# Attention, then a two-layer MLP with split f16 products: the first batch's attention in groups of two units, w_out's bit conversion ahead of the token norms, w_out's scale later, some blocks one step later

## The chip, the cores and the metric

The kernel runs on one core of a Trainium2 chip. A core has a matrix engine (TensorE, "PE" in the profile, with "PEld" for its weight loads), a vector engine (VectorE, "DVE"), a scalar engine (ScalarE, "ACT"), GpSimd ("POOL") and SyncE ("SP", here used to issue DMAs). Each engine works off its own instructions in order; they wait for each other through semaphores. Matmul results go to PSUM, of which this program names the slots "sc" (two of two banks), "mm" (two), "av" and "tr" (one each).

The metric is device time of one execution in microseconds, the median of several runs. Lower is better.

## The reference

```python
scores = scale * np.matmul(q, k.transpose(0, 1, 3, 2)) - np.log(S)
attn = 1.0 / (1.0 + np.exp(-scores))            # a sigmoid, no softmax
attn_out = np.matmul(attn, v)
x = attn_out.transpose(0, 2, 1, 3).reshape(B * S, H * D)
h = x @ w_in
g = h - np.tanh(h)
out = g @ w_out
```

Batch 8, 12 heads, 448 tokens of 64 dimensions each; so x is 3584 x 768, w_in 768 x 2048, w_out 2048 x 768. The weights come as float64 and are converted on the chip.

## The kernel before, in words

**Stages.** Batches are worked one after the other. Batch 0 is special: its attention (`attention32`) and its first MLP product (`moe1_32`) use f32 operands while the weights are still being loaded and converted. Later batches use pairs of f16 (a high and a low half, three products each) in `moe1` and `moe2`. While one batch's second product (`moe2`) runs, the next batch's attention is fed in between as "blocks" of a generator (`stream`).

**Units.** Heads are treated in six pairs j. A unit (j, c) is one slice of 128 key tokens (c = 0, 1, 2) of a pair; c = QT = 3 is the rest of 64 tokens for two pairs at once, so even pairs have four units and odd ones three, 21 in all. A unit is `scores` (PE, into a slot "sc"), `weigh` (sigmoid on ACT, a 128 x 896 tile) and `av` (PE, times v, into an accumulator). When a pair is done `evac_x` copies the accumulator (ACT for even pairs, DVE for odd ones), ACT squares it, POOL adds the squares.

**attention32 before (L625 to L645).** A loop over the 21 units: scores, weigh, then the av of the unit two before, then one step of `weights` (two after a rest unit).

**weights and rest.** Both are generators made by `convert` (L178). A piece of a weight matrix passes through load (SP's DMA), sign (ACT, `conv_sign`), bits (three DVE operations, `conv_bits`, L151 to L155) and end (one PE matmul, `conv_end`, L168 or L172). Each `next` runs one step: every stage for another piece, from the last stage to the first. `weights` is w_in in 24 pieces of 512 KB (five buffers "raw"; the end of a piece comes one step after its bits). The first `rest` is half of w_out in 16 pieces of 384 KB (the end comes two steps after the bits); a second `rest` with the other half runs in batch 0's `moe2`.

**moe1_32 (L741 to L783).** For k = 0 to 7 and e = 0, 1: twelve f32 matmul instructions into "ph" (slot "sc"), then the small things of that step: at (0, 0) the last of `weights`, the token norms (`token_norms`: two matmuls "nm", a DVE reduction); at (0, 1), (1, 0), (1, 1) the sums that give w_in's scale (`w_in_scales`); one `next(self.blocks)` at e = 0 (INIT); then steps of `rest`. After e = 1 comes `mix`: u and th on ACT, then five DVE operations with ACT's squares between (L791 to L809). The last k's mix is left to `first`, which runs it in steps (`tail`) between the first five blocks of batch 1's attention. `w_out_scale(0)` (eight DVE operations, L248 to L255) is issued at the end of moe1_32, ahead of that last mix.

**Blocks.** For two pairs (g, g + 1) there are five blocks: units 0 and 1 of g; units 2 and 3 of g and the norms (ACT squares "sqn") of pair g + 3's q and k; the sums of those norms on PE ("pbn", L297) with the scales and the next K; units 0 and 1 of g + 1; unit 2 of g + 1. BLOCKS0 and BLOCKS1 say after which step of `moe2` a block is issued, for the passes of batch 0 and of batch 1. A step is six matmuls "po" of 384 columns. BLOCKS is the same list for later batches.

**What sets the order.** PE, ACT, DVE and POOL are in a manual schedule: they execute in program order. SP is in it from batch 1 on; in all of batch 0 the framework orders SP's DMA issues by itself. `manual_schedule` leaves the choice of slots and the waits to the framework.

Of the kernel before, what the change touches and what calls it, by code (L numbers as in the profile page):

```python
# [20 lines left out]
D = 64  # L21
QT = 3
# [11 lines left out]
class Builder:  # L34
# [7 lines left out]
    BLOCKS = (8, 11, 16, 19, 20, 24, 27, 32, 35, 36, 40, 43, 48, 51, 52)  # L42
    TAIL = (1, 2, 3, 4, 5)
    ALONE = 11
    BLOCKS0 = (2, 5, 7, 8, 12, 16, 20, 22, 24, 31, 38)
    BLOCKS1 = (4, 6, 7, 10, 13, 16, 19, 20, 24, 27, 32, 35, 36, 40, 43, 48, 51, 52)

    TP = 8
    SHIFT = 4
# [534 lines left out]
    def attention32(self, b, weights, rest):  # L584

        nc = self.nc
        S = self.S
        NP = self.NP
        xs = []
        tags = (("kn", "qn"), ("K", "Q"))  # L590
        self.row = []
        loaded = {}

        def load(j):
            loaded[j] = self.load_qk(b, j, tags[j % 2])
            if j < 2:
                next(weights)
            loaded[j].append(self.load_v(b, j, self.att, "vhl", 3))

        load(0)  # L600
        one = self.sm.tile([P, 1], F32, name="one", tag="m")
        nc.scalar.activation(one, self.nls, AF.Sigmoid)
        next(weights)
        load(1)
        next(weights)
        todo = []
        accs = {}

        def open_acc(j):
            accs[j] = self.ps.tile([P, 512], F32, name="acc", tag="mm", bufs=2)  # L610

        def av():
            j, c, a = todo.pop(0)
            v = loaded[j][2][:, None]
            if c == QT:
                open_acc(j + 1)
                self.av([accs[j], accs[j + 1]], v, a, c, 0)
            else:
                if c == 0 and j % 2 == 0:
                    open_acc(j)  # L620
                self.av([accs[j]], v, a, c, j % 2)
            if c == (QT, QT - 1)[j % 2]:
                xs.append(self.evac_x(j, accs.pop(j), None))

        self.warm(12)  # L625
        order = [(j, c) for j in range(NP) for c in (range(QT) if j % 2 else range(QT + 1))]
        for n, (j, c) in enumerate(order):
            both = (j, j + 1) if c == QT else (j,)
            ps = self.scores([loaded[i][0][:, None] for i in both], [loaded[i][1][:, None] for i in both], c)
            todo.append((j, c, self.weigh(ps, 1.0 / math.sqrt(D))))  # L630
            if n < 2:
                self.warm(4)
            if len(todo) > 2:
                av()
            if c == 1 and j + 2 < NP:
                load(j + 2)
            next(weights)
            if c == QT:
                next(weights)
            if n == len(order) - 1:  # L640
                next(rest)
        while todo:
            av()
            next(weights, None)
            next(rest)  # L645
        self.xs = xs

    def token_norms(self, nm):
# [92 lines left out]
    def moe1_32(self, xs, weights, rest):  # L741


        nc = self.nc
        S = self.S
        self.gs = []
        self.late = []
        for k in range(self.NF // 2):
            ph = self.ps.tile([P, 2, 512], F32, name="ph", tag="sc", bufs=2)
            for e in range(2):  # L750
                f = 2 * k + e
                for c in range(self.NC):
                    nc.tensor.matmul(  # L753
                        ph[:, e, :S],
                        self.where("in", c)[:, f * P : (f + 1) * P],
                        xs[c],
                        start=(c == 0),
                        stop=(c == self.NC - 1),
                    )
                if k == 0 and e == 0:  # L760
                    for _ in weights:
                        pass
                    w = self.w_in_scales()
                    m = self.token_norms(self.ps.tile([P, 512], F32, name="nm0", tag="mm", bufs=2))
                elif k < 2:
                    next(w, None)
                if (k, e) == (1, 1):
                    self.Sg, self.iSg = self.g_scales(m)
                if e == 0 and k in self.INIT:
                    next(self.blocks)  # L770
                for _ in range(3 if k == 0 else 1):
                    next(rest, None)
                if (k, e) == (self.NF // 2 - 1, 1):
                    for _ in rest:
                        pass
                    self.w_out_scale(0)
            g = self.gp.tile([P, 2, 2, S], F16, name="g", tag="g")
            self.gs.append(g)
            self.tail = self.mix(ph[:, :, :S], g, self.ih0, self.ihk0)
            if k == self.NF // 2 - 1:  # L780
                return
            for _ in self.tail:
                pass  # L783
# [140 lines left out]
    def first(self, rest):  # L924

        n = 5
        next(self.tail)
        ahead = [self.split_w_out(0)]
        for k in range(n - 1):
            if k == 2:  # L930
                next(self.blocks)
            next(self.blocks)
            for _ in range(2):
                next(self.tail, None)
            if k == 1:
                next(ahead[0])
            if k == 2:
                self.finish_g()
                next(ahead[0])
        next(ahead[0])  # L940
        next(rest)
        next(ahead[0])
        next(rest)
        assert n + len(self.BLOCKS0) + len(self.BLOCKS1) == 5 * self.NP + len(self.BLOCKS) - self.ALONE
        split = self.split_w_in()
        at, each = self.SPLIT
        events = [(at + k * each, lambda: next(split, None)) for k in range(self.NC * self.NB + 1)]
        events += [(k + 0.5, lambda: next(ahead[0], None)) for k in range(self.NF // 2 - 3)]
        steps = self.NF + 4
        events += [(k * self.CONV, lambda: next(rest, None)) for k in range(1, steps + 1)]  # L950
        at = math.ceil(steps * self.CONV)

        def scale():
            self.w_out_scale(1)
            ahead[0] = self.split_w_out(1)

        events += [(at, scale)] + [(at + 0.5 * k, lambda: next(ahead[0], None)) for k in range(1, self.NF // 2 + 1)]
        self.second(0, self.BLOCKS0, len(self.BLOCKS0) - 1, events)

    def batch(self, b):  # L960
# [15 lines left out]
        if b == 1:  # L976
            alone += len(self.BLOCKS1) - len(self.BLOCKS)
            blocks = self.BLOCKS1
        self.second(b, blocks, alone, events)
# [56 lines left out]
```

## Time and profile before

| | us |
|---|---|
| median of 3 runs | 1209.24 (1207.33 to 1209.73) |
| the profiled execution | 1209.36 |
| its span, first to last instruction | 1207.6 |
| batch 0's attention, first scores to first ph | 6.42 to 58.98 |
| moe1_32, first ph to the first scores of batch 1 | 58.98 to 139.77 |
| busy in the span: PE, DVE, ACT | 1171.3, 917.9, 872.5 |
| mean granted TensorE clock | 0.991 |

A row of the timeline has the start, the duration, engine, line of the program, operation, output tile <- input tiles, shape and count; behind it in brackets, how long the engine was idle before and what it was waiting for. Consecutive equal instructions are merged into a row, so a row's duration is that of its whole run, and matmuls overlap: the pace of PE is read from start to start.

### The profile page before, as it was taken

How to read it: one execution, taken by the hardware profiler on the slowest of the kernel's cores; microseconds unless marked ns; L12 is line 12 of the kernel's file. 1: busy time of each engine (PE TensorE's matmuls, PEld its weight loads, DVE VectorE, ACT ScalarE, POOL GpSimd, SP SyncE). 2: the span in 40 equal slices, each digit the busy share in tenths (PEclk: the TensorE clock that was granted, in tenths of full speed). 3: DMA queues.
4: the chain of work that ended last, by engine and by line, in shares of the span. 5: the costliest groups of instructions: out<-in, count | busy, mean ns of one | idle time of the engine just before them, and what ended most of it. 6: DMA issues, size and time to landing. Idle time of an engine off the chain costs nothing.

```text
span 1207.6 us, 19052 instructions
## 1 busy us (share of the span) xinstructions
PE 1171.3 (97%) x7581; PEld 602.4 (50%) x7581; DVE 917.9 (76%) x1362; ACT 872.5 (72%) x1219; POOL 81.6 (7%) x62
## 2 busy tenths in 40 slices
PE   9899869899999999999999999999999999999998
PEld 2244324455445555555555555555555555555555
DVE  6879888779876798678976798668977789646930
ACT  6757787958888588867878688886887688844820
POOL 0100000000011000110011000210003000210000
PEclk9999899999999999999999999999999999999999
DMA  9832145100022100211012100221002100000000
GB/s 337 303 102 77 46 148 157 59 21 1 18 82 66 51 1 16 73 60 38 1 53 75 57 2 16 66 67 37 1 29 84 60 14 1 29 19 15 1 14 33
DMA packets 34057, 70.43 MB, mean 58 GB/s; under 512 B 3888, under 2 KB 21040, under 8 KB 33968
## 3 DMA queue, kind: packets, MB, share of 16 engines
q1 hardware_dynamic: 33824, 68.99, 17.9%
q8 instruction: 59, 0.97, 0.3%
q14 instruction: 30, 0.25, 0.1%
q10 hardware_dynamic: 144, 0.23, 0.1%
HBM read 58.20 MB, written 11.01 MB: 57 GB/s over the span
## 4 chain that ended last, share of the span: by engine, by line
PE 85%; DVE 7%; ACT 4%; issue 3%; DMA 1%; DVEq 0%; ACTq 0%; SPq 0%
PE ph L723 31%; PE po L836 29%; PE sc L347 8%; PE acc L378 7%; PE por L874 5%; PE ph L753 3%; DMA raw<-moe_w_in 1%; ACT a L358 1%; DVE stb L152 1%; DVE m L795 1%; PE warm L91 1%; DVE g L708 1%; DVE m L806 1%; DVE stb L151 1%; DVE wo L203 1%
## 5 line engine op out<-in xcount | busy, mean ns | idle before, releaser
L836 PE MATMUL po<-wo,g 128*128 128x384 f16 x2304 | 396.4, 327 | 3.2 <-DVE wo L203 1.2
L723 PE MATMUL ph<-xhl,wi 128*128 128x448 f16 x2016 | 382.6, 352 | 0.0
L836 PEld LDWEIGHTS <-g 128*128 128x128 f16 x2304 | 220.2, 99 | 174.1 <-issue 35.9
L723 PEld LDWEIGHTS <-wi 128*128 128x128 f16 x2016 | 196.7, 98 | 185.0 <-issue 1.8
L365 DVE SCALAR_TENSOR_TENSOR ahl<-a,ahl 128x896 f16<-128x896 f32 x126 | 160.6, 1309 | 135.2 <-ACT ahl L364 135.1
L358 ACT ACTIVATE a<-sc,nls,rn 128x896 f32<-128x896 f32 x147 | 156.3, 1091 | 51.3 <-PE sc L347 47.7
L791 ACT ACTIVATE u<-ph,ih 128x896 f32<-128x896 f32 x64 | 64.4, 1006 | 83.3 <-PE ph L723 79.1
L364 ACT ACTIVATE ahl<-a 128x896 f16<-128x896 f32 x126 | 113.1, 940 | 0.6
L347 PE MATMUL sc<-Q,K 64*128 64x448 f16 x1008 | 104.2, 362 | 4.6 <-DVE th L796 2.3
L795 DVE SCALAR_TENSOR_TENSOR m<-ph,ihk,u 128x896 f32<-128x896 f32 x64 | 73.4, 1147 | 29.2 <-ACT th L793 28.8
L707 ACT ACTIVATE g<-m,Sg 128x896 f16<-128x896 f32 x64 | 66.6, 1041 | 36.1 <-DVE m L809 29.1
L809 DVE COPY_PREDICATED m<-u,th 128x896 f32<-128x896 uint32 x64 | 77.1, 1205 | 6.6
L378 PE MATMUL acc<-ahl,vhl 128*64 128x448 f16 (+1 forms) x864 | 81.3, 358 | 0.0
L708 DVE SCALAR_TENSOR_TENSOR g<-m,Sg,g 128x896 f16<-128x896 f32 x64 | 73.3, 1145 | 8.5 <-ACT g L707 8.5
L406 POOL TENSOR_TENSOR x<-x 128x448 f32<-128x448 f32 x24 | 26.4, 1100 | 769.4 <-ACT x L394 769.4
L806 DVE SCALAR_TENSOR_TENSOR m<-q,m 128x896 f32<-128x896 f32 x64 | 69.9, 1093 | 10.8 <-ACT q L805 3.8
L753 PE MATMUL ph<-x,wi 128*128 128x448 f32 x192 | 74.8, 539 | 0.0
L796 DVE SCALAR_TENSOR_TENSOR th<-ph,ih,th 128x896 f32<-128x896 f32 x64 | 73.2, 1143 | 0.0
L808 ACT ACTIVATE u<-u,b 128x896 f32<-128x896 f32 x64 | 66.7, 1043 | 7.3 <-DVE m L795 5.3
L802 DVE SCALAR_TENSOR_TENSOR m<-q,m 128x896 f32<-128x896 f32 x64 | 69.5, 1085 | 0.0
L347 PEld LDWEIGHTS <-K 64*128 64x128 f16 x1008 | 36.4, 98 | 65.0 <-issue 40.4
L874 PE MATMUL por<-wo,g 128*64 128x384 f16 x768 | 65.8, 327 | 1.1 <-ACT o L865 1.1
(127 smaller groups left out, 1154.0 us busy)
## 6 DMA issues: line engine op xcount, KB each, us to landing
raw<-moe_w_in SPq DMA_DIRECT2D x24, 512.0 KB, 6.1
rawo<-moe_w_out SPq DMA_DIRECT2D x32, 384.0 KB, 3.8
knn<-k SPq DMA_DIRECT2D x45, 224.0 KB, 2.5
qnn<-q SPq DMA_DIRECT2D x44, 224.0 KB, 2.6
out<-o SPq DMA_DIRECT2D x21, 384.0 KB, 2.3
vn<-v SPq DMA_DIRECT2D x24, 256.0 KB, 2.9
vn<-v SPq DMA_DIRECT2D x24, 192.0 KB, 2.4
out<-orem SPq DMA_DIRECT2D x16, 96.0 KB, 2.2
```

Of the source, the lines that this page charges most:

```text
L347: self.nc.tensor.matmul(ps[i * m : (i + 1) * m, h, : self.S], K[i][r, w, c * P : c * P + m], Q[i][r, x, :], start=(n == 0), stop=(n == len ...
L358: self.nc.scalar.activation(a[:, 0], ps[:, :, : self.S], AF.Sigmoid, bias=self.nls, scale=scale)
L364: nc.scalar.activation(A[:, 0], a[:, 0], AF.Copy, scale=A_SCALE)
L365: nc.vector.scalar_tensor_tensor(A[:, 1], a[:, 0], A_SCALE, A[:, 0], op0=ALU.mult, op1=ALU.subtract)
L378: self.nc.tensor.matmul(acc[i][h * D : (h + 1) * D, : self.S], v[k, w, 2 * QT + h if half else h * QT + c], A[k, x, h], start=(n == 0 and ...
L708: nc.vector.scalar_tensor_tensor(g[:, 1], m, Sg, g[:, 0], op0=ALU.mult, op1=ALU.subtract)
L723: nc.tensor.matmul(ph[:, e, :S], self.wi[:, c * self.NB + k, part, e * P : (e + 1) * P], xhl[c][:, x, :], start=(i == 0), stop=(i == 3 * s ...
L753: nc.tensor.matmul(ph[:, e, :S], self.where("in", c)[:, f * P : (f + 1) * P], xs[c], start=(c == 0), stop=(c == self.NC - 1),)
L795: V.scalar_tensor_tensor(m, ps, ihk, u, op0=ALU.mult, op1=ALU.mult)
L806: V.scalar_tensor_tensor(m, q2, C2, m, op0=ALU.add, op1=ALU.mult)
L836: nc.tensor.matmul(po[i][:, :H], gs[f // 2][:, x, f % 2, tk * P : (tk + 1) * P], self.wo[:, i * self.NF + f, w], start=(f == 0 and n == 0) ...
L874: nc.tensor.matmul(po[e * D : (e + 1) * D, :H], gs[f // 2][:, x, f % 2, nm:S], self.wo[:, e * self.NF + f, w], start=(f == 0 and n == 0), ...
```

## The change

attention32 takes two units at a time: both scores, both weighs, then all av that were ready before this group (two, none in the first group), then the steps of `weights` of both units. The last group has one unit. After the loop comes one step of `rest`, the last av, and two steps of `rest`, so three as before; the 29th step of `weights` (the end of piece 23) is no longer made here but with "the last of `weights`" in moe1_32.

In moe1_32 the steps of `rest` come directly behind the ph matmuls, ahead of the last of `weights`, the token norms, w_in's sums and the block; and there are two per half at k = 0 instead of three. `w_out_scale(0)` moves behind the first step of the last mix.

In BLOCKS0 the steps 7, 8 and 22 become 8, 9 and 23; in BLOCKS1 6, 7 and 10 become 7, 8 and 11.

```diff
-    BLOCKS0 = (2, 5, 7, 8, 12, 16, 20, 22, 24, 31, 38)
-    BLOCKS1 = (4, 6, 7, 10, 13, 16, 19, 20, 24, 27, 32, 35, 36, 40, 43, 48, 51, 52)
+    BLOCKS0 = (2, 5, 8, 9, 12, 16, 20, 23, 24, 31, 38)
+    BLOCKS1 = (4, 7, 8, 11, 13, 16, 19, 20, 24, 27, 32, 35, 36, 40, 43, 48, 51, 52)
...
-        for n, (j, c) in enumerate(order):
-            both = (j, j + 1) if c == QT else (j,)
-            ps = self.scores([loaded[i][0][:, None] for i in both], [loaded[i][1][:, None] for i in both], c)
-            todo.append((j, c, self.weigh(ps, 1.0 / math.sqrt(D))))
-            if n < 2:
+        for n in range(0, len(order), 2):
+            group = order[n : n + 2]
+            pss = []
+            for j, c in group:
+                both = (j, j + 1) if c == QT else (j,)
+                K, Q = ([loaded[i][x][:, None] for i in both] for x in range(2))
+                pss.append(self.scores(K, Q, c))
+            ready = len(todo)
+            todo += [(j, c, self.weigh(ps, 1.0 / math.sqrt(D))) for (j, c), ps in zip(group, pss)]
+            if n < 4:
                 self.warm(4)
-            if len(todo) > 2:
+            for _ in range(ready):
                 av()
-            if c == 1 and j + 2 < NP:
-                load(j + 2)
-            next(weights)
-            if c == QT:
+            for j, c in group:
+                if c == 1 and j + 2 < NP:
+                    load(j + 2)
                 next(weights)
-            if n == len(order) - 1:
-                next(rest)
+                if c == QT:
+                    next(weights)
+        next(rest)
         while todo:
             av()
-            next(weights, None)
             next(rest)
+        next(rest)
...
                         stop=(c == self.NC - 1),
                     )
+                for _ in range(2 if k == 0 else 1):
+                    next(rest, None)
                 if k == 0 and e == 0:
                     for _ in weights:
                         pass
...
                 if e == 0 and k in self.INIT:
                     next(self.blocks)
-                for _ in range(3 if k == 0 else 1):
-                    next(rest, None)
                 if (k, e) == (self.NF // 2 - 1, 1):
                     for _ in rest:
                         pass
-                    self.w_out_scale(0)
...
         next(self.tail)
+        self.w_out_scale(0)
         ahead = [self.split_w_out(0)]
```

## The prediction

> **What bounds the kernel now.** I read the page's first line and its slices, then a table of windows, then the waits of PE, then the order of time at the places that those name.
>
> ```profile
> span 1207.6 us, 19052 instructions
> ```
>
> ```profile
> 15.37:32.56 17.19, 15.72 (x74) 4.17 (x73) 15.16 (x26) 13.35 (x20) 1.37 (x1) 1.00 0.98 352
> 32.56:49.74 17.18, 15.71 (x74) 4.17 (x73) 15.93 (x26) 14.67 (x21) 2.61 (x2) 1.00 0.91 331
> 59.00:139.77 80.77, 77.33 (x223) 38.35 (x221) 71.26 (x114) 52.98 (x75) 0.00 (x0) 1.00 0.30 85
> 500.00:600.00 100.00, 100.00 (x691) 52.70 (x686) 79.92 (x113) 76.26 (x100) 5.98 (x4) 1.00 0.12 36
> ```
>
> Columns of a window: width, then busy time of PE, PEld, DVE, ACT, POOL, the granted clock, DMA share, GB/s. From about 225 us on PE has no gap worth the name (100.00 of 100), so whatever is won or lost earlier arrives at the end one for one. All that the change touches lies before 330 us. There PE is nearly full too, but so is DVE: in batch 0's attention (two periods of seven units, 17.19 and 17.18 us) DVE is idle only 2.03 and 1.25 us.
>
> ```profile
> PE pbn L297 <- ACT sqn L289: 8.2, 3, 3.8
> PE wl L168 <- DVE stb L152: 8.1, 9, 1.4
> PE cs L172 <- DVE sta L152: 3.3, 3, 1.4
> PE sc L347 <- DVE th L796: 2.3, 1, 2.3
> ```
>
> Total, number of times, longest. These four are what the edits can reach: 21.9 us at most, and 8.2 of it is the sums of norms (pbn) standing in PE's queue before ACT has the squares.
>
> **The change part by part.** First the groups of two in attention32.
>
> ```profile
> 39.12 1.02 PE L347 MATMUL sc<-qnn,knn 64*128 64x448 f32 x4
> 40.08 0.97 PE L378 MATMUL acc<-a,vn 128*64 128x448 f32 x4
> 40.98 0.40 PE L172 MATMUL cs<-sta,identb 128*128 128x512 bf16 x1
> 41.31 1.02 PE L347 MATMUL sc<-qnn,knn 64*128 64x448 f32 x4
> ...
> 80.68 4.67 PE L753 MATMUL ph<-x,wi 128*128 128x448 f32 x12
> 85.19 0.33 PE L168 MATMUL wl<-stb,onesb 128*128 128x384 bf16 x1
> ```
>
> Start to start, scores take 0.96, attention times v 0.90 and cs 0.33: 2.19 us per unit. Twelve f32 matmuls in a row take 4.51, or 0.376 each; four that run two by two would need 0.75. So a change of kind costs up to 0.21 after scores and 0.15 after av, and pairing removes one of each per group: 0.36, in ten groups 3.6 us of PE time. The rows before show no pair of f32 units, so 0 to 3.6 are the bounds of what PE can save. The Trainium skill (TensorEngine Tiling (Array Packing), Key Properties) says that changing the tiling mode drains the TensorE, which names the same gap; by it the sum would be rival 1.
>
> I take it that PE does not collect this, because DVE sets the pace:
>
> ```profile
> 17.39 0.66 ACT L146 ACTIVATE sta<-raw 128x512 f32<-128x512 f32 x1 [1.77 <-DMA raw<-moe_w_in]
> 20.30 0.54 ACT L392 ACTIVATE x<-acc 128x448 f32<-128x448 f32 x1
> 20.88 0.58 ACT L404 ACTIVATE x<-x 128x448 f32<-128x448 f32 x1
> ...
> 18.08 0.43 DVE L151 TENSOR_SCALAR sta<-sta 128x512 uint32<-128x512 uint32 x1 [0.56 <-ACT sta L146]
> 22.52 0.43 DVE L151 TENSOR_SCALAR sta<-sta 128x512 uint32<-128x512 uint32 x1 [0.77 <-ACT sta L146]
> 31.04 0.42 DVE L151 TENSOR_SCALAR sta<-sta 128x512 uint32<-128x512 uint32 x1
> 32.83 0.42 DVE L151 TENSOR_SCALAR sta<-sta 128x512 uint32<-128x512 uint32 x1
> 53.59 0.42 DVE L151 TENSOR_SCALAR sta<-sta 128x512 uint32<-128x512 uint32 x1
> ...
> 58.98 4.78 PE L753 MATMUL ph<-x,wi 128*128 128x448 f32 x12
> ```
>
> One piece of w_in costs DVE 1.79 us (31.04 to 32.83), and PE's cs for a piece needs its bits. Up to piece 5 (18.08) the arrival of the raw weights decides (1.77 us wait at 17.39), with groups or without. From there to piece 22 (53.59) DVE takes 35.5 us, of which I put 1.5 down as idle, between the 0.77 of the row at 22.52 and the 3.3 of the two windows together. In groups, the sign of a piece stands on ACT behind two weighs (0.9 each) and, where an accumulator ends, behind its copy and square (20.30, 20.88: 1.05 together). Walked group by group with a group's PE time of 3.9 us (sc 1.70, av 1.65, cs 0.57), DVE finds nothing to do for 1.6 us at piece 6 (sign ends 17.95 + 2 x 0.9 + 1.05 + 0.65 = 21.5, DVE free at 19.9), 0.65 at the first copy, 0.8 and 0.3 in the middle and 1.3 at piece 22: 4.65 instead of 1.5. Piece 22 then starts at 53.6 + 3.1 = 56.7; its second operation ends 1.15 later, cs and the last av (0.33 + 0.96) end at 59.1. Against 58.98 that is **0**; the last cs, now behind the next stage's first half, no longer makes PE wait here. Bounds: -4.1 us (PE's 3.6 and the 0.5 of the last wait) and +3.
>
> Second, w_out's bits and the small sums in moe1_32. T is the start of the first ph, 58.98.
>
> ```profile
> 64.17 0.62 DVE L652 TENSOR_REDUCE m<-nm 128x1 f32<-128x448 f32 x1 [4.45 <-PE nm L650]
> 72.55 0.35 DVE L151 TENSOR_SCALAR stb<-stb 128x384 uint32<-128x384 uint32 x1
> 74.01 1.15 DVE L795 SCALAR_TENSOR_TENSOR m<-ph,ihk,u 128x896 f32<-128x896 f32 x1
> ...
> 142.10 0.54 DVE L248 TENSOR_REDUCE mo<-wl 128x1 f32<-128x384 f32 x1
> 143.63 1.13 DVE L795 SCALAR_TENSOR_TENSOR m<-ph,ihk,u 128x896 f32<-128x896 f32 x1
> 151.69 1.09 DVE L806 SCALAR_TENSOR_TENSOR m<-q,m 128x896 f32<-128x896 f32 x1 [3.81 <-ACT q L805]
> ...
> 139.77 0.74 PE L347 MATMUL sc<-Q,K 64*128 64x448 f16 x6
> ...
> 145.88 2.57 PE L347 MATMUL sc<-Q,K 64*128 64x448 f16 x18 [2.31 <-DVE th L796]
> ```
>
> Before, DVE sits idle for 4.45 us ahead of the token norms and then does five pieces of bits (1.46 each, 72.55 to 74.01) before the first mix, at T + 15.0. After, one piece fills part of that idle time and two follow, so the first mix waits only for PE and ACT: two halves of ph (2 x 4.51), cs and nm (0.7), and u on ACT (about 1): T + 11. But two pieces (2.9 us) are left for later. DVE is otherwise solid from 74.01 to 142.10 (68.1 us), so the last mix starts at T + 11 + 68.1 + 2.9 + 0.5 (one wait for W2's sum) = T + 82.5. Before it was T + 84.65, because w_out_scale stood ahead of it (142.10 to 143.63, 1.53 us). th's end releases the PSUM that the waiting scores need (145.88). That is 2.1 us earlier; the unit behind it then waits for the weigh in between, so I take **-1.8**. w_out_scale itself is hidden: behind th, DVE waits 3.81 us for ACT a little later (151.69), and the split that needs the scale comes after. If that cover were gone it would cost its 1.53. What is late next: the last piece's wl now follows the last ph on PE and waits for bits behind the sixth mix, T + 77 to T + 82; that is time in which PE had little else. SP gets the same loads two steps later, each with over 4 us of PE work to land in. Bounds -2.5 and +1.4 (the scores start 1.4 later, T + 82.2 for the T + 80.8 of the row at 139.77, and all behind them too).
>
> Third, the blocks moved by one step.
>
> ```profile
> 174.41 1.14 PE L836 MATMUL po<-wo,g 128*128 128x384 f16 x6
> ...
> 179.68 0.59 PE L297 MATMUL pbn<-ss,onesf 128*128 128x4 f32 x2 [2.59 <-ACT sqn L289]
> ...
> 214.44 0.39 PE L297 MATMUL pbn<-ss,onesf 128*128 128x6 f32 x2 [3.84 <-ACT sqn L289]
> ...
> 323.03 0.39 PE L297 MATMUL pbn<-ss,onesf 128*128 128x6 f32 x2 [1.79 <-ACT sqn L289]
> ```
>
> The squares belong to the block before, which stays; so ACT is ready at the same time and one step of po (six matmuls, 1.14 us in the row at 174.41, about 1.0 where the next follows at once) is drawn into each wait: 2.59 to about 1.3 (its wl comes along), 3.84 to 2.8, 1.79 to 0.8. Sum **-3.3**. What waits behind pbn (scale, then K and Q of the next pair on ACT and DVE) is late by a step of splits; three to seven steps of po lie between it and its reader. If not, a step's 1.0 comes back, at each place.
>
> Fourth, the granted clock.
>
> ```profile
> 170.94:174.35 3.41, 1.98 (x21) 0.96 (x20) 2.72 (x5) 3.38 (x8) 1.14 (x1) 1.00 0.45 120
> 174.35:177.76 3.41, 1.52 (x8) 0.58 (x6) 3.31 (x8) 1.57 (x3) 0.00 (x0) 1.00 0.01 4
> 321.13:324.53 3.40, 1.61 (x11) 0.84 (x12) 2.26 (x3) 3.40 (x7) 0.00 (x0) 1.00 0.01 2
> 324.55:327.95 3.40, 3.40 (x20) 1.33 (x18) 3.30 (x10) 2.40 (x5) 0.00 (x0) 0.50 0.02 5
> ```
>
> After stretches in which PE was busy 1.52 and 1.61 of 3.4 us the clock fell to 0.50; after one with 1.98 it did not. With 0.8 us of waiting at 323 PE is busy about 2.6 of 3.4, and the 3.40 us at half clock go, of which half is lost: **-1.7**. At 178 and 214 the waits that are left, with those beside them, still reach 1.4 to 2.8 us; there I count nothing. The Trainium skill (TensorE: Matmul & The Clock Gate, Why this matters for your kernels) asks only that no idle gap exceed about 3 us; the trace disagrees, since one wait of 1.79 was enough. By that page this term would be 0 and the sum 1204.3, inside the forecast's own range below.
>
> Sum: 0 - 1.8 - 3.3 - 1.7 = -6.8. The profiled execution took 1209.36 (span 1207.6 and 1.76 around it), 0.12 over the median of the runs shown: 1209.36 - 6.8 = **1202.6**.
>
> **The rivals.** (1) PE paces the attention, DVE keeps up. For it: the gaps between kinds in the rows above, and 2.03 and 1.25 us of slack on DVE per period. Against: that slack is all there is. It gives 4.1 more: 1198.5. (2) The moved blocks don't do what they say: the wait is for ACT, and what is drawn ahead makes PE run into bits that DVE hasn't done (the wl row, 8.1 us in nine waits, is in just that stretch), so the term of 3.3 shrinks to about 0.5 and the clock still falls. 1209.36 - 1.8 - 0.5 = 1207. (3) Slower: ACT's order in the groups. If every sign comes a weigh (0.9) too late for DVE in all ten groups, and the five with an accumulator's copy and square lose 1.05 each as well, that is 9.0 + 5.2 = 14.2 us of idle less about 3 that is there now: +11.2, and 1209.36 + 11.2 - 6.8 = 1213.8. It decides as soon as DVE drains its queue before 3.5 us into a group; by my walk it drains at 4.2.
>
> **How the numbers follow.** Forecast (1200.5 to 1205) 0.50; rival 1 0.20; rival 2 0.18; rival 3 0.08; 0.04 elsewhere. The range takes in rival 1 with a us to spare and rival 2: 1197 to 1208. A measurement of this kernel can tell about 0.2% (2.4 us) from no change. Faster than 1206.8: the forecast, rival 1 and about half of rival 2, 0.79; within 0.2%: 0.13; slower: 0.08.
>
> **What would show it.** Right: the first f32 ph starts at 58 to 60; DVE's idle time in the attention, ended by ACT, rises to some 4 us, while scores come in rows of eight; the first mix starts 11 us behind that ph; th of the last mix ends 1.5 to 2.5 us earlier relative to it; pbn waits fall to about 1.3, 2.8 and 0.8; clock 1.00 behind 324. Wrong: a first ph at 55 (rival 1), pbn waits unchanged or new wl waits beside them (rival 2), a first ph at 64 or later (rival 3). What I can't see is the order of SP's loads, which the program doesn't write out here; raw weights that come later would move everything.

## The result, and the profile after

The changed kernel takes 1213.96 us (median of five runs, 1212.76 to 1215.83) against 1209.24 for the kernel before. The ratio is 1.0048 (95% interval 1.0031 to 1.0065): **slower by 0.5%**, where 1202.6 was predicted. The profiled execution is the longest of the five, 1215.83, and its span stands against 1207.6 before:

```profile
span 1214.1 us, 19039 instructions
```

In the prediction's order, first what the tensor engine waits for (total us, times, longest):

```profile
PE wl L168 <- DVE stb L152: 8.3, 5, 5.1
PE cs L172 <- DVE sta L152: 7.6, 9, 1.9
PE pbn L297 <- ACT sqn L289: 6.5, 4, 2.4
PE acc L378 <- ACT tn L299: 4.8, 1, 4.8
```

The sums of norms (pbn) wait less than before, 6.5 for 8.2. But cs waits 7.6 for 3.3, one wl alone waits 5.1, and the last row is new: an accumulator that waits 4.8 us for tn, ACT's reader of pbn.

To place them, cut the span at four instructions of PE: the first f32 ph (T), the first po, the third pbn shown in the prediction (214.44 before), and the first po behind the av that follows it (222.92 before). PE's order of time in the kernel after has these points, and the rows around them (start, duration, instruction, and in brackets its wait):

```profile
63.26 4.78 PE L758 MATMUL ph<-x,wi 128*128 128x448 f32 x12
...
145.86 0.48 PE L168 MATMUL wl<-stb,onesb 128*128 128x384 bf16 x1 [5.11 <-DVE stb L152]
146.27 1.30 PE L347 MATMUL sc<-Q,K 64*128 64x448 f16 x6
148.76 3.62 PE L347 MATMUL sc<-Q,K 64*128 64x448 f16 x24 [1.19 <-ACT a L358]
...
164.33 1.15 PE L840 MATMUL po<-wo,g 128*128 128x384 f16 x6
...
185.09 0.39 PE L297 MATMUL pbn<-ss,onesf 128*128 128x4 f32 x2 [1.14 <-ACT sqn L289]
186.44 2.08 PE L840 MATMUL po<-wo,g 128*128 128x384 f16 x6 [0.96 <-ACT oh L859]
...
217.81 0.39 PE L297 MATMUL pbn<-ss,onesf 128*128 128x6 f32 x2 [2.42 <-ACT sqn L289]
218.06 1.14 PE L840 MATMUL po<-wo,g 128*128 128x384 f16 x6
219.13 1.31 PE L347 MATMUL sc<-Q,K 64*128 64x448 f16 x12
225.23 5.95 PE L378 MATMUL acc<-a,vn 128*64 128x448 f32 x20 [4.79 <-ACT tn L299]
231.11 7.00 PE L840 MATMUL po<-wo,g 128*128 128x384 f16 x42
...
331.21 0.39 PE L297 MATMUL pbn<-ss,onesf 128*128 128x6 f32 x2 [0.82 <-ACT sqn L289]
```

| stretch | before | after | difference |
|---|---|---|---|
| start to T | 58.98 | 63.26 | +4.28 |
| T to first po | 99.93 | 101.07 | +1.14 |
| first po to pbn | 55.53 | 53.48 | -2.05 |
| pbn to po behind av | 8.48 | 13.30 | +4.82 |
| from there to the end | 984.65 | 982.95 | -1.70 |

The sum is +6.49, the difference of the two spans. Two stretches gain, about what the moved blocks and the clock were to give. Three lose, and the largest lies at the one block that moved from step 22 to 23. The losses were taken up one by one.

### The profile page after: what moved, and what is told of

Same layout as the page of the kernel before. It is cut to its first block, busy times and chain, and to the rows that moved or that the text cites. A ratio compares the mean times of both kernels' runs of the same rounds, so it can differ in the third digit from the quotient of the medians.

```text
span 1214.1 us, 19039 instructions
## 1 busy us (share of the span) xinstructions
PE 1171.2 (96%) x7580; PEld 604.0 (50%) x7581; DVE 917.7 (76%) x1362; ACT 872.0 (72%) x1219; POOL 81.5 (7%) x62
## 4 chain that ended last, share of the span: by engine, by line
PE 70%; ACT 1%; DVE 0%; issue 0%; ACTq 0%; DVEq 0%
PE ph L728 27%; PE po L840 26%; PE sc L347 6%; PE acc L378 6%; PE por L878 5%; ACT a L358 0%; DVE ahl L365 0%; PE pbn L297 0%; ACT ahl L364 0%; ACT o L869 0%; PE nm L655 0%; ACT sqn L289 0%; ACT x L394 0%; ACT Q L322 0%; DVE orem L887 0%
## 5 line engine op out<-in xcount | busy, mean ns | idle before, releaser
L347 PEld LDWEIGHTS <-K 64*128 64x128 f16 x1008 | 36.7, 99 | 66.0 <-issue 42.0
```

The lines of the kernel that those rows point to most:

```text
L347: self.nc.tensor.matmul(ps[i * m : (i + 1) * m, h, : self.S], K[i][r, w, c * P : c * P + m], Q[i][r, x, :], start=(n == 0), stop=(n == len ...
```

## The experiments

Theory A: three independent losses. (1) The block at step 23 leaves pbn in the PSUM slot av so late that the next block's accumulator, which opens in av, must wait for ACT to read it. (2) Two steps of w_out's bits for three at k = 0 make the last wl, and batch 1's scores behind it, wait. (3) Groups of two make cs wait for signs. Rival B: groups of two alone, that is, T. Rival C: the granted clock alone.

Most kernels are the kernel after with one edit undone, or the kernel before with one edit alone. The points in time are those of a kernel's one profiled execution; the ratios are against the kernel before on the same chip.

| kernel | ratio (95%) | T | first scores of batch 1 - T | first po - T |
|---|---|---|---|---|
| before | 1 | 58.98 | 80.79 | 99.93 |
| after | 1.0048 (1.0031 to 1.0065) | 63.26 | 83.01 | 101.07 |
| e1: after, block 22 | 1.0005 (0.9992 to 1.0018) | 59.87 | 83.00 | 101.08 |
| e2: after, unit by unit | 1.0025 (1.0014 to 1.0036) | 58.88 | 82.78 | 100.87 |
| e3: after, three steps | 0.9998 (0.9989 to 1.0007) | 59.69 | 78.28 | 96.53 |
| e4: before + groups | 1.0026 (1.0016 to 1.0035) | 59.76 | 80.99 | 100.14 |
| e5: before + blocks, 22 kept | 0.9980 (0.9971 to 0.9990) | 58.89 | 80.82 | 99.94 |
| e6: before + block 23 | 1.0037 (1.0023 to 1.0051) | 58.66 | 80.72 | 99.88 |
| e9: after, pbn in slot tr | 1.0002 (0.9993 to 1.0011) | 61.60 | 82.81 | 100.86 |
| e11: before + scale later | 0.9993 (0.9983 to 1.0002) | 58.34 | 80.80 | 99.74 |
| e12: before + order, three steps | 0.9987 (0.9977 to 0.9997) | 60.94 | 78.03 | 97.77 |
| e8: e3 + e2 + e1 | 0.9948 (0.9935 to 0.9960) | 58.69 | 78.06 | 96.27 |
| e13: e8 + groups, sign first | 0.9956 (0.9943 to 0.9969) | 59.67 | 78.24 | 96.67 |
| e14: e8 + block 23, pbn in tr | 0.9955 (0.9938 to 0.9972) | 59.22 | 78.03 | 96.26 |

### The block at step 23 (e1, e6, e9)

First undone, in the kernel after:

```diff
-    BLOCKS0 = (2, 5, 8, 9, 12, 16, 20, 23, 24, 31, 38)
+    BLOCKS0 = (2, 5, 8, 9, 12, 16, 20, 22, 24, 31, 38)
```

> The changed kernel with one block put back from step 23 to step 22 of batch 0's moe2. My theory: with the block at 23 only one step of po lies between pbn and the next block's attention times v; that one opens its accumulator in the PSUM slot 'av', in which pbn lies until ACT has read it (tn), and tn stands behind ACT's splits of w_out. So the 4.79 us wait of acc for ACT tn goes (under 0.5 left), the half clock behind it (223.7 to 230.5) goes too, the pbn wait at about 218 grows from 2.4 to about 3.8, and the time falls by 4 to 6 us, to 1208 to 1210. Rival: tn is late because batch 0's conversions all come late in this kernel, wherever the block stands; then acc still waits over 3 us and the time stays within 1.5 us of 1214.

Then alone, in the kernel before:

```diff
-    BLOCKS0 = (2, 5, 7, 8, 12, 16, 20, 22, 24, 31, 38)
+    BLOCKS0 = (2, 5, 7, 8, 12, 16, 20, 23, 24, 31, 38)
```

> The kernel before with the one block moved from step 22 to 23, nothing else. My theory: pbn waits 1 us less (3.84 to 2.8), but a wait of acc for ACT tn of 3 to 5 us appears behind it, and the time rises by 3 to 5 us to 1212 to 1214. Rival (my prediction's step): nothing that reads the sums is near, and the time falls by about 1 us.

And kept at 23, with the sums of norms in another PSUM slot (in every block that isn't an early one):

```diff
-            scales(g + 2, "mm" if early else "av")
+            scales(g + 2, "mm" if early else "tr")
```

> The changed kernel, with the sums of norms (pbn, block three of a pair) in the PSUM slot 'tr' instead of 'av'; the block stays at step 23. My theory says that attention times v waits for the slot 'av' until ACT's tn has read pbn. In 'tr' pbn is in the way of the odd head pair's accumulator only, which the fourth of the four waiting units opens; so the first three units (12 of the 20 matmuls, 2.5 to 3 us) run while tn is still late, the single wait of 4.79 shrinks to about 2, in the middle of the av, and the time falls by 2.5 to 4 us. Rival: what av waits for is ACT's order (tn merely the last thing before), not the slot; then the wait of 4.8 stands where it stood and the time stays within 1.5 us of 1214.

e1 brings the time back to 1.0005, 4.3 parts in a thousand or about 5 us below the kernel after; the accumulator no longer waits, and pbn waits 3.42. e6 costs 3.7 in a thousand by itself, with pbn waiting 2.83 and the accumulator 3.73. Both loss and place are thus shown. What the wait is made of stands in ACT's order of time, first before, then after:

```profile
219.13 0.25 ACT L299 ACTIVATE tn<-pbn,tiny 128x6 f32<-128x6 f32 x1
```

```profile
222.50 0.50 ACT L200 ACTIVATE wi<-wi,swi_s 128x256 f16<-128x256 f32 x1
222.90 2.12 ACT L200 ACTIVATE wo<-wo,swo_s 128x384 f16<-128x384 f32 x4
224.93 0.25 ACT L299 ACTIVATE tn<-pbn,tiny 128x6 f32<-128x6 f32 x1
```

The splits of the weights stand ahead of tn in ACT's queue. Before, tn ended at 219.38 and the accumulator in PE's order started at 219.60 with no wait:

```profile
219.60 3.39 PE L378 MATMUL acc<-a,vn 128*64 128x448 f32 x20
```

After, one step of po fewer lies between pbn and that accumulator, and one step of splits more (the rows at 222.50 and 222.90) lies between pbn and tn. A wait that had been hidden by 0.2 us became 4.79. The clock makes it dearer: it was granted at 0.50 from 223.7 to 230.5, and after the wait the twenty matmuls take 5.95 for 3.39.

In e9 tn ends as late behind pbn as that, but the accumulators no longer have to wait for it from their start. PE's rows, then ACT's:

```profile
216.05 0.58 PE L297 MATMUL pbn<-ss,onesf 128*128 128x6 f32 x2 [2.42 <-ACT sqn L289]
...
220.22 4.22 PE L378 MATMUL acc<-a,vn 128*64 128x448 f32 x20
```

```profile
223.16 0.25 ACT L299 ACTIVATE tn<-pbn,tiny 128x6 f32<-128x6 f32 x1
```

acc starts 2.94 us before tn and without a wait, with the block still at 23; the time is 1.0002. Yet its twenty matmuls take 4.22 us for 3.39 at a granted clock of 1.00. A row that merges instructions shows no wait that falls inside it; this one is seen at the weight loads (PEld), where the last of them, those of the odd pair's accumulator, stand behind tn:

```profile
223.47 0.20 PEld L378 LDWEIGHTS acc<-a,vn 64*64 64x64 f32 x4 [0.65 <-ACT tn L299]
```

So the wait moves to the odd accumulator, as was expected, and costs some 0.8 us, less than the 2 expected and far less than 4.79. What made step 23 dear is thus the slot: theory A's first loss holds, and rivals B and C, which left this block out, don't carry the result.

### Two steps of w_out's bits for three (e3, e12)

In the kernel after:

```diff
-                for _ in range(2 if k == 0 else 1):
+                for _ in range(3 if k == 0 else 1):
                     next(rest, None)
```

> The changed kernel with three steps of rest per half at k = 0 instead of two, still right behind the ph matmuls. My theory: the two steps that were taken away there put the last piece's bits behind the sixth mix on DVE, so that its wl, now PE's last matmul before batch 1's scores, waits 5.11 us and the scores start late, at half clock. With three steps the 5.11 is under 1 us, the first scores of batch 1 start 77.5 to 81 us behind the first f32 ph instead of 83.0, the first po 99 to 100 us behind it instead of 101.1, and the time falls by 1 to 2.5 us. Rival: DVE's sum is the limit there and the wl wait is free, since the scores wait for th of the last mix anyway: the first po stays at 101 behind the first ph and the time within 0.7 us.

And the kernel before, in which only these rest steps (three at k = 0) stand right behind the ph matmuls, as in the kernel after:

```diff
+                for _ in range(3 if k == 0 else 1):
+                    next(rest, None)
                 if k == 0 and e == 0:
...
-                for _ in range(3 if k == 0 else 1):
-                    next(rest, None)
```

> The kernel before with the three and one steps of rest right behind the ph matmuls, ahead of the token norms, w_in's sums and the block, and nothing else. My theory: DVE's idle 4.45 us ahead of the token norms is filled with bits, the first mix starts 12 to 13 us behind the first ph for 15.0, and as DVE is solid from there to the last mix, the first po comes 1.5 to 2.5 us earlier (97.5 to 98.5 behind the first ph for 99.9); the time falls by 1.5 to 2.5 us. Rival: it is w_out_scale's place that won e3_three its 3.4 us, and the order is worth under 0.7.

e3 is the largest single gain over the kernel after, 5.0 in a thousand. PE's order of time in e3:

```profile
137.97 0.74 PE L347 MATMUL sc<-Q,K 64*128 64x448 f16 x6
...
156.22 1.15 PE L840 MATMUL po<-wo,g 128*128 128x384 f16 x6
...
217.31 4.87 PE L378 MATMUL acc<-a,vn 128*64 128x448 f32 x20 [3.21 <-ACT tn L299]
```

The last wl no longer waits; batch 1's first scores start at T + 78.3 instead of T + 83.0, and the first po at T + 96.5 instead of T + 101.1. What sets the first po is one of two things. One is the end of the last mix's th, which releases the PSUM that waiting scores need. DVE's rows for it, before and in e3:

```profile
144.69 1.13 DVE L796 SCALAR_TENSOR_TENSOR th<-ph,ih,th 128x896 f32<-128x896 f32 x1
```

```profile
141.94 1.17 DVE L800 SCALAR_TENSOR_TENSOR th<-ph,ih,th 128x896 f32<-128x896 f32 x1
```

The first po follows this end by 13.1 us before, and by 13.1 to 13.3 in e3 to e6, e8 and e12 to e14. The other is the start of the first scores: in the kernels where the last wl has made them late (after, e1, e2, e9) no scores wait for th any more, and the first po follows the first scores by 18.1 us (18.05 to 18.09), and th's end by 15.7 to 15.8. The wait for tn is still there in e3 (3.21), as e3 keeps block 23. e12 has the order alone, and th's end and the first po both come 2.2 us earlier, about two thirds of e3's 3.4, so the rival (that the scale's place won these) is out; its time is 0.9987, with a T that a half-clock window (33.3 to 36.7) had put late.

### w_out's scale alone (e11)

```diff
# end of moe1_32
-                    self.w_out_scale(0)
# first
         next(self.tail)
+        self.w_out_scale(0)
```

> The kernel before with w_out_scale(0) behind the tail's first step, nothing else. My theory: th of the last mix ends 1.5 us earlier (85.3 us behind the first f32 ph for 86.85), the second wait of the scores shrinks by as much, and the first po comes 0.8 to 1.5 us earlier: time lower by 0.5 to 1.5 us, at the edge of what can be told. Rival: the scale, now later, delays the split of w_out and the first po does not move.

th of the last mix ends at T + 85.33 for T + 86.84 before, the 1.5 us of the small sums, and the scores' wait for it falls from 2.31 to 0.68. First scores stay at T + 80.8. The last av before the first po starts 1.0 us earlier (T + 98.04 for T + 99.02), but the first po itself only 0.2: a half-clock window lies there in this execution (granted clock 0.50 from 156.4 to 159.8) and that av takes 1.76 us for 0.97. So the trace shows the gain of 0.8 to 1.5 that was expected and loses most of it to the clock; the time, 0.9993 (0.9983 to 1.0002), isn't told from no change.

### Groups of two (e2, e4, e13)

e4 puts the loop of the change, as it stands in the diff, into the kernel before; e2 puts the loop of before into the kernel after.

> The kernel before with the groups of two alone. My theory: they cost 4 us by themselves: first f32 ph at 62 to 64 against 58.98, with PE waits for bits of w_in of 6 to 8 us in all (3.3 before) and one or two stretches at half clock before 60 us; the time is 1212 to 1214. Rival: the groups cost nothing alone, and the late first ph of the changed kernel comes from the rest steps around them: first ph at 58 to 60, time 1209.

> The changed kernel with batch 0's attention unit by unit as before; all else as changed. My theory: groups of two make DVE wait for signs that stand behind two weighs on ACT, PE then waits at the group's end for bits, and twice the clock falls to one half (36.0 to 39.4, 53.1 to 56.5). Unit by unit the clock stays at 1.00 up to 140 us, the first f32 ph starts at 58.5 to 59.5 instead of 63.3, and the time falls by 4 us, to about 1210. Rival: the raw weights land later in the changed kernel because SP's loads come in another order, and groups have no part in it: first ph still at 62 or later.

Taking the groups out wins 2.3 in a thousand, putting them in loses 2.6: some 3 us either way. In e4 the waits for bits come as expected (7.6 us), but T is 59.76 and the clock is full through the attention, as the rival had it. PE does collect what pairing was to save. In its order of time after:

```profile
24.40 1.77 PE L347 MATMUL sc<-qnn,knn 64*128 64x448 f32 x8
26.11 1.72 PE L378 MATMUL acc<-a,vn 128*64 128x448 f32 x8
27.76 0.40 PE L172 MATMUL cs<-sta,identb 128*128 128x512 bf16 x1
...
35.05 0.39 PE L172 MATMUL cs<-sta,identb 128*128 128x512 bf16 x1 [1.40 <-DVE sta L152]
...
52.97 0.54 PE L172 MATMUL cs<-sta,identb 128*128 128x512 bf16 x1 [1.88 <-DVE sta L152]
```

Start to start, eight scores take 1.71 where twice four took 1.92, and eight av 1.65 for 1.80. The Trainium skill (TensorEngine Tiling (Array Packing), Key Properties) says that a change of tiling mode drains the engine; the trace agrees, with 0.21 and 0.15 us a change. The gain goes into the waits for bits, 7.6 us in nine of them. DVE for its part waits for signs that ACT issues late. Its longest such row after the first piece, which stands behind a stretch at half clock (53.05 to 56.46, below); in e1, e3 and e4, where the clock is full there, the same wait is 1.5:

```profile
60.35 0.92 DVE L151 TENSOR_SCALAR sta<-sta 128x512 uint32<-128x512 uint32 x1 [3.14 <-ACT sta L146]
```

In e4 PE's order ends the attention so:

```profile
58.55 0.39 PE L172 MATMUL cs<-sta,identb 128*128 128x512 bf16 x1 [0.37 <-DVE sta L152]
58.86 0.97 PE L378 MATMUL acc<-a,vn 128*64 128x448 f32 x4
59.76 4.78 PE L758 MATMUL ph<-x,wi 128*128 128x448 f32 x12
```

T is 59.7 to 59.9 in e1, e3 and e4, and 58.3 to 59.2 in the kernels without groups whose clock is full up to there, so by this the groups cost some 0.9 us. In the kernel after T was 63.26 with the same attention; the other 3.4 is the clock. Windows of the kernel after (width; busy PE, PEld, DVE, ACT, POOL; granted clock; DMA share, GB/s):

```profile
32.57:35.98 3.41, 1.84 (x9) 0.64 (x9) 3.31 (x6) 1.34 (x3) 0.00 (x0) 1.00 0.92 349
35.98:39.39 3.41, 3.41 (x16) 0.72 (x12) 3.18 (x6) 2.58 (x3) 0.00 (x0) 0.50 0.87 281
49.64:53.05 3.41, 1.36 (x7) 0.21 (x3) 2.89 (x6) 1.72 (x4) 0.00 (x0) 1.00 0.86 299
53.05:56.46 3.41, 3.41 (x9) 1.18 (x8) 3.31 (x6) 1.68 (x2) 0.00 (x0) 0.50 0.88 305
```

and of e1:

```profile
33.04:36.45 3.41, 1.89 (x8) 0.78 (x9) 3.27 (x7) 1.94 (x4) 0.00 (x0) 1.00 0.87 313
36.45:39.86 3.41, 3.41 (x22) 0.86 (x20) 2.65 (x5) 3.32 (x6) 0.44 (x1) 1.00 0.94 289
```

Two windows of 3.41 us at half clock lose up to 1.7 each, which is the 3.4. Same code, windows cut at other instants: 1.84 of 3.41 busy, and the clock halves; 1.89, and it holds. In e3 and e4 the same stretch has 1.84 as well (from 32.61 and 32.69), and the clock holds there too. It fell on the attention in two of six traces with groups (after, e9) and in one of eight without (e12, 33.3 to 36.7, T 60.94), too few to say that groups bring it on. Of executions without a trace the record has the mean granted clock, though not where it fell: 0.9897 in the nine of e4, 0.9910 in the 28 of before beside them, which is one half-clock window more in e4, or up to 1.7 us (an estimate from these means). But e2 without groups (0.9905) and the kernel after with them (0.9900) hardly differ, nor do e8 (0.9912) and e13 (0.9918). So of the 3 us that the times give the groups, some 0.9 are explained; whether the clock is the rest stays open.

e13 tries to mend the groups: in e8 with groups, the first unit's step of weights, and with it ACT's sign, goes ahead of the two weighs (`steps` holds the loads and the steps of `weights` of one unit).

```diff
             ready = len(todo)
+            steps(*group[0])
             todo += [(j, c, self.weigh(ps, 1.0 / math.sqrt(D))) for (j, c), ps in zip(group, pss)]
...
-            for j, c in group:
-                if c == 1 and j + 2 < NP:
-                    load(j + 2)
-                next(weights)
-                if c == QT:
-                    next(weights)
+            for j, c in group[1:]:
+                steps(j, c)
```

> e8_best with the groups of two put back, but the first unit's step of w_in (cs, bits, sign, load) ahead of the two weighs and av, so that on ACT a sign stands behind at most one weigh pair's half. My theory, that groups lose because signs come late for DVE: DVE's idle time ended by signs falls from 8 us (e1_no23) to under 5, no half clock before 60 us, first f32 ph at 57 to 58.7, time equal to e8_best or up to 1.5 us lower. Rival: the raw weights' loads set DVE's pace; then ACT waits longer for raw, its weighs with it, and the first ph stays at 59.5 or later, the time 1 to 3 us above e8_best.

It decides nothing: the time, 0.9956, can't be told from e8's 0.9948 without groups, T is 59.67, and DVE waits for signs as long as in e4 (11.0 us for 11.3, with some 5.4 ahead of the first piece in both). A sign that stands earlier in ACT's queue now waits itself. ACT's row in e13:

```profile
53.71 0.66 ACT L146 ACTIVATE sta<-raw 128x512 f32<-128x512 f32 x1 [3.51 <-PE acc L378]
```

The bracket names PE's attention times v, but in the program that stands behind this sign. The chain of work that ends there names the raw weights: their load was issued at 46.46 and took 7.14 us, to 53.60. That is the rival's course, and T is as late as it said; its loss of 1 to 3 us against e8 isn't seen.

### The other blocks (e5), and the versions that beat both (e8, e14)

```diff
-    BLOCKS0 = (2, 5, 7, 8, 12, 16, 20, 22, 24, 31, 38)
-    BLOCKS1 = (4, 6, 7, 10, 13, 16, 19, 20, 24, 27, 32, 35, 36, 40, 43, 48, 51, 52)
+    BLOCKS0 = (2, 5, 8, 9, 12, 16, 20, 22, 24, 31, 38)
+    BLOCKS1 = (4, 7, 8, 11, 13, 16, 19, 20, 24, 27, 32, 35, 36, 40, 43, 48, 51, 52)
```

> The kernel before with the other moved blocks alone (steps 8 and 9 for 7 and 8 of batch 0's moe2; 7, 8, 11 for 6, 7, 10 of batch 1's). My theory: two of the three pbn waits shrink by about 1 us each (2.59 to 1.3, 1.79 to 0.8), the half clock at 324 to 328 goes (another 1.7), and the time falls by 2 to 4 us. Rival: what is drawn ahead waits for w_out's bits instead, only batch 1's part is won: 1 to 2 us.

These moves gain 2.0 in a thousand (1.0 to 2.9). PE's rows in e5 show one of the waits and what comes back behind it:

```profile
179.59 0.39 PE L297 MATMUL pbn<-ss,onesf 128*128 128x4 f32 x2 [1.13 <-ACT sqn L289]
...
180.95 1.14 PE L836 MATMUL po<-wo,g 128*128 128x384 f16 x6 [0.98 <-ACT oh L855]
```

2.59 has become 1.13, and the next po now waits 0.98 for ACT to empty its accumulator (oh).

e8 is the kernel after with the loop unit by unit (e2), three steps (e3) and block 22 (e1). e14 is e8 with block 23 and pbn in tr (e9).

> The changed kernel with three of its edits taken back or mended: batch 0's attention unit by unit, three steps of rest per half at k = 0, the block at step 22. What stays is the place of the rest steps, w_out_scale behind the tail's first step, and the blocks at 8 and 9 and in batch 1. Expected by adding the parts up: first f32 ph at 58.9, first po 96.5 behind it (e3_three) and so at 155.4 against 158.9 before, no acc wait for ACT tn, clock 1.00 at 324; 1201 to 1205. If the parts don't add (DVE's backlog or ACT takes it back in batch 0's moe2), 1205 to 1208.

> e8_best with the block at step 23 after all and pbn in the slot 'tr'. With the slot out of the way (e9_tr) the later block should win what I predicted for it: pbn waits 1 us less (3.46 to about 2.4), no acc wait for ACT tn, time 0.5 to 1.5 us under e8_best. Rival: the odd accumulator then waits for tn in place of the even one and the time is equal to e8_best or above it.

e8: 0.9948 (0.9935 to 0.9960), e14: 0.9955 (0.9938 to 0.9972), **both faster than before** by half a per cent, 1203.51 and 1202.34 us. They can't be told from each other. In e14 pbn waits 2.42 for e8's 3.46, and its accumulators take 4.21 us for 3.39, the odd one behind tn as in e9 (0.6 us at its weight loads): what the later step wins there is given back, as the rival had it. PE's points in e8:

```profile
58.69 4.78 PE L753 MATMUL ph<-x,wi 128*128 128x448 f32 x12
...
136.75 0.74 PE L347 MATMUL sc<-Q,K 64*128 64x448 f16 x6
...
154.96 2.05 PE L835 MATMUL po<-wo,g 128*128 128x384 f16 x7
```

The single undoings add up to 4.3 + 5.0 + 2.3 = 11.6 in a thousand; all three together gave 10.0. From the other side, groups +2.6, block 23 +3.7, the other blocks -2.0 and the scale -0.7 make +3.6 of the +4.8. The rest, 1.2, would be the two-step order, which was not run by itself; the +1.14 us at the first po is of that size, and so is what these intervals leave uncertain.

## Why the prediction was wrong

**Attention, predicted 0: mis-sized.** The walk was near on DVE, whose order in e4 has piece 22 so:

```profile
56.85 0.91 DVE L151 TENSOR_SCALAR sta<-sta 128x512 uint32<-128x512 uint32 x1 [1.49 <-ACT sta L146]
57.80 0.69 DVE L152 SCALAR_TENSOR_TENSOR sta<-raw,sta 128x512 uint32<-128x512 uint32 x1
```

It was to start at 56.7, and the last cs did move behind the first half of ph without a wait. But the first operation took 0.91 where 0.42 was counted, so the bits came 1.64 after that start, not 1.15, and T at 59.8, not 59.1. And the clock was left out: I kept it at 1.00 through a stage in which PE was to wait more often, which in the profiled execution cost 3.4. The bound of +3 was about what the times give; it entered the chances as rival 3 alone, and that by a harsher mechanism. Rival 3's 1213.8 lies next to the measured 1213.96, but not for its reason: its 11.2 us of further idle time on DVE did not come (in e4 the waits for signs are 11.3 us for 8.9 before, 2.4 more), and undoing block 23 or the two steps each wins more than undoing the groups (4.3 and 5.0 in a thousand by e1 and e3, 2.3 by e2). That it came close is luck.

**w_out's bits, predicted -1.8: the step that failed is "that is time in which PE had little else".** The first mix was to start at T + 11 and th to end 1.5 to 2.5 earlier. DVE's order of time after (T = 63.26):

```profile
75.13 1.15 DVE L799 SCALAR_TENSOR_TENSOR m<-ph,ihk,u 128x896 f32<-128x896 f32 x1 [0.71 <-ACT th L797]
...
146.31 1.15 DVE L799 SCALAR_TENSOR_TENSOR m<-ph,ihk,u 128x896 f32<-128x896 f32 x1
147.37 1.14 DVE L800 SCALAR_TENSOR_TENSOR th<-ph,ih,th 128x896 f32<-128x896 f32 x1
```

T + 11.9, and the last mix at T + 83.05 for T + 84.65: th is 1.6 earlier, right as far as it goes. But the 5.11 us of the last wl stand ahead of batch 1's scores in PE's queue. They start 2.2 later than before, not the 1.4 that was the upper bound, and in this kernel what follows hangs on them and not on th. The choice of th itself was sound: where the last wl doesn't wait, the first po follows th's end by 13.1 us, and by that (an estimate) th's 1.6 would have been 1.6 at the first po, near the 1.8 forecast. What failed is the wl wait, which the prediction saw coming and put at nothing. With three steps the same edits give -3.4 at th and at the first po (e3: 96.53 for 99.93).

**Blocks, predicted -3.3: the step that failed is "three to seven steps of po lie between it and its reader".** The waits at pbn fell as predicted, to 1.14, 2.42 and 0.82 for 1.3, 2.8 and 0.8. What I followed was the reader of the scales, K and Q of the next pair. The instruction in the way was the next user of pbn's PSUM slot, one step behind, and the reader that it waits for was in ACT's queue behind a step of splits. My price for being wrong, "a step's 1.0 comes back", was too low as well: the wait alone is 4.79. Without block 23 the moves gain (e5); the 0.96 for oh is a small return that the prediction did not have.

**Clock at 324, predicted -1.7: right in kind, but before has that window only in part of its executions.** The window after:

```profile
324.00:332.00 8.00, 7.18 (x55) 3.72 (x53) 6.74 (x8) 7.93 (x13) 0.00 (x0) 1.00 0.00 1
```

The last stretch, which holds it, gained 1.70, of the 2.7 that the clock and the shorter pbn wait were to give. e11 and e12 keep before's blocks and its pbn wait there (1.79 and 1.78), and their clock held all the same. Of the five traces with before's blocks in batch 1, three (before, e4, e6) have a half-clock window there; of the nine with the moved blocks none has. So the moved block does seem to take it away, but the 1.7 is there to be won only in some executions.

Rival 2 named the right kind of event, PE drawn ahead into a wait, but let it do no more than shrink the gain. None of the three had a buffer's next user in it.

## What to carry to other kernels

Where a step is moved in a queue written by hand, look up not only who reads its result but who next opens the buffer that it lies in, and what stands ahead of that reader in its own engine's queue. A wait that is said to fall in free time has to be checked against what stands behind the waiting instruction in the same queue: here it was the next stage's first scores. Of several edits sent together, run each alone and each undone: the same change without three of its choices is 0.5% faster than before instead of 0.5% slower.

## What the runs showed of the hardware

Between the start and the end of these traces all half-clock stretches are one to three windows of 3.41 us, laid on a fixed grid whose phase differs from one execution to the next. The Trainium skill (TensorE: Matmul & The Clock Gate, What's actually happening) describes a free-running window of 3413 ns, and the traces agree. What decides is not a long gap. Up to 340 us of the fourteen traces, every window at full clock with PE busy 1.43 us or less of the 3.41 was followed by one at half clock, and none with 1.87 or more. Between them it went either way: 1.45 (e9, from 137.59) kept the clock and 1.86 (e12, from 29.88) lost it, so the busy share of one window, as these records show it, doesn't decide alone. Once at half clock, windows with up to 3.03 us busy were followed by another at half. Single waits of 1.4 to 1.9 us, in windows with other small gaps, were enough (the rows at 35.05 and 52.97 above), where the Trainium skill (TensorE: Matmul & The Clock Gate, Why this matters for your kernels) allows idle gaps of about 3.
